# Gated linear attention into a squared-ReLU MoE: the transposes of the last six chunks moved from TensorE to DMAs on SyncE's queue, and a longer lead of the chunks over the MoE

## The chip, the cores and the metric

The kernel runs on one core of a Trainium2 chip. The metric is the device time of one launch in microseconds. Before the change the median of three runs is 194.05 us (193.65 to 194.7). The profiled execution took 194.29 us, and its profile spans 192.3 us from the first to the last instruction.

## The reference

Two stages follow each other. The first is a recurrence per batch and head, over 768 steps; the state is a 48 x 48 matrix:

```python
def _attn_ref(q, k, v, alpha):            # each 4 x 8 x 768 x 48
    state = np.zeros((B, H, D, D))
    for t in range(S):
        state = alpha[:, :, t, :, None] * state + np.einsum('bhd,bhe->bhde', k[:, :, t], v[:, :, t])
        y[:, :, t] = np.einsum('bhd,bhde->bhe', q[:, :, t], state)
    return y
```

Its result, with the heads side by side, is a matrix x of 3072 tokens by 384. The second stage is

```python
    h = x @ w_in                          # 384 x 2048
    r = np.maximum(h, 0.0)
    out = (r * r) @ w_out                 # 2048 x 384
```

Inputs and output are float32. alpha lies between 0.8 and 1.

## The kernel before

**Chunks.** The recurrence is computed in 24 chunks of 128 tokens, six for each batch, in `add_chunk(s)`. Four loads of 192 KB bring alpha, q, k and v of a chunk (line 296). ScalarE (ACT) takes the logarithm of alpha (L, line 318). TensorE (PE) multiplies it by a triangular matrix of ones, which gives cumulative sums, and adds the chunk's totals (`e_p0`, line 326). ACT makes the exponentials A and 1/A of the sums (lines 345 and 349). VectorE (DVE) makes qA = q * A (line 370) and kI = k / A (line 373) in bf16, each 128 tokens by 8 heads padded to 64 columns.

For the scores, channels have to lie on partitions, so qA and kI are transposed: four 128 x 128 transposes on PE for each, into one PSUM bank (`e_p1q`, `e_p1k`, lines 377 to 387, through the helper `tr`, line 223), and one DVE copy of 1024 columns from PSUM into the tile `qkT` (line 397; the first four chunks do it in halves on DVE or ACT). Eight score matmuls follow (`e_p2`, line 402, into the PSUM tile `sc`), DVE masks them in two instructions (line 414, tile `sm`), PE adds the part that comes from the state (`e_p3a`) and the part within the chunk (`e_p3b`, lines 442 to 455), ACT copies the result to bf16 (`xn`, line 463), PE transposes it in three pieces (`e_p4`, line 467), and DVE copies these into `xT_big` (line 474), which holds x transposed for all tokens. From kI, not from its transpose, PE updates the state (`e_ps`, line 420), DVE scales it (line 434) and ACT copies it (line 439). The scratch for L, qA and kI has four buffers (`NBUF`), so a chunk's logarithm waits for the chunk four before to be at its end (`old`, line 305). The loads have six buffers (`LB`): a load waits until the instruction that used its buffer six chunks before is done.

**MoE.** Tokens go in twelve groups (`GN`: 4, 1, 1, then 2 chunks each). For each group and each of 16 slices of d_ff, PE does three matmuls (`add_moe1`; 256 columns for two chunks), ACT the ReLU (line 513) and DVE the square (line 520, tile `gT`). Then for each chunk of the group 16 matmuls of 384 columns in four quarters (`add_moe2`, line 532), a copy by ACT or DVE (`ob`, lines 549 and 551) and a store of 192 KB (line 556). All matmuls stand at line 220, all transposes at line 223, as both go through a helper.

**What sets the order.** Every step is an `Op` with an engine, a duration and a latency that the author wrote down, and its dependences. `Plan.run` (lines 96 to 136) fills the engines in model time: it picks what can start first, and by priority among equals. The resulting list, sorted by start, is emitted in that order, and each engine executes its instructions in that order. PSUM banks are part of the model: two banks go to the chunks (`GLA_BANKS`), two or three to the first MoE matmul, one or more to the second. An operation on PE that depends on another engine gets a slack of 0.25 us in the model once PE is past 25 us (lines 75 to 77). Stores are emitted 3.5 us later than the model's time (`OUT_LATE`), so that they don't hold up SP. Loads and stores are all issued on SyncE's (SP's) queue, in order; the weights come on GpSimd's (POOL's).

How far chunks may run ahead of the MoE is set by `gate` (line 601): a chunk's cumulative sum may be placed when

```python
            return s <= LEAD + (prog["m1"] + prog["m2"]) / 5.12
```

where the fraction is the MoE work placed so far, in chunks, and `LEAD` is 3.5. There are 24 loads of each kind and eight completion semaphores that DMAs on SP take in turn.

Of the kernel before, what the change touches and what calls it, by code (L numbers as in the profile page):

```python
# [9 lines left out]
BF16 = mybir.dt.bfloat16  # L10
# [44 lines left out]
def after(op, x=0.0):  # L55
    return (op, x)


class Plan:
# [36 lines left out]
    def run(self, gate):  # L96
        free = self.free
        while any(self.pending.values()):
            best = None
            for eng, ops in self.pending.items():  # L100
                t0 = free.get(eng, 0.0)
                pick = None
                fifo = eng in ("DMA",)
                for op in (ops[:1] if fifo else ops):
                    if not gate(op):
                        continue
                    r = self.ready(op)
                    if r is None:
                        continue
                    if len(op.durs) > 1:  # L110
                        ends = {e: max(r, free.get(e, 0.0)) + x + LAT[e] for e, x in op.durs.items()}
                        if ends[eng] > min(ends.values()):
                            continue
                    key = (max(r, t0), op.prio)
                    if pick is None or key < pick[0]:
                        pick = (key, op)
                if pick is not None and (best is None or pick[0][0] < best[0]):
                    best = (pick[0][0], eng, pick[1])
            assert best is not None, "nothing can run"
            t, eng, op = best  # L120
            for e in op.durs:
                self.pending[e].remove(op)
            op.eng, op.dur = eng, op.durs[eng]
            op.start = t + getattr(op, "late", 0.0)
            free[eng] = t + op.dur
            if op.lat is None:
                op.lat = LAT.get(eng, 0.2)
            if eng == "OUT":
                free["DMA"] = max(free.get("DMA", 0.0), t) + op.dur
            op.done = t + op.dur + op.lat  # L130
            if op.takes is not None:
                self.ready(op)
                op.slot.release.append(op.gives if op.gives is not None else op)
            self.order.append(op)
            self.on_pick(op)
        self.order.sort(key=lambda o: o.start)
# [3 lines left out]
def kernel(  # L140
# [10 lines left out]
    nc = tc.nc  # L151
    B, H, S, D = q.shape
    HD = H * D
    P = 128
    DP = 64
    NP = H // 2
# [17 lines left out]
    work = ctx.enter_context(tc.tile_pool(name="work", bufs=4))  # L174
# [18 lines left out]
        out=utri_f, in_=utri_f, compare_op=ALU.is_ge, fill=0.0,  # L193
# [20 lines left out]
    xT_big = big.tile([P, KT, n_tok], BF16)  # L214

    def pin(ins):
        tc.keep_in_program_order(ins)
# [4 lines left out]
    def tr(*a):  # L222
        pin(nc.tensor.transpose(*a))  # L223

    plan = Plan()
# [5 lines left out]
    GLA_BANKS = sl_bank[0:2]  # L231
    SIDE_BANKS = sl_bank[2:4]
# [6 lines left out]
    X_SLACK = 0.2  # L239
    LD = 0.93  # L240
    LD_LATE = 1.05
    WLD = 2.05
    SQ_PRIO = 0.0

    def add(eng, dur, emit, *deps, **kw):
        return plan.add(Op(eng, dur, emit, deps, **kw))
# [6 lines left out]
    def load_w(which):  # L253
# [9 lines left out]
        issue = add("POOL", W_ISSUE, e_issue, w_gate[0], prio=-3.0, lat=0.4)  # L263
        w_ready[which].append(add("DMA", WLD * (hi - lo) / 4, lambda: None, issue, lat=2.2))

# [21 lines left out]
    EARLY = 4  # L287

    def add_load(s, nm):
# [7 lines left out]
        prev = C[s - LB]["use_" + nm] if s >= LB else None  # L297
        d["ld_" + nm] = add("DMA", LD if s < 6 else LD_LATE, ld, prev, d.get("go") if nm == "at" else None, lat=2.0 if s < 4 else 2.4, at=0.6)

    def add_chunk(s):  # L300
        d = C[s]
        b, c = divmod(s, NCH)
        i = s % NBUF
        L, qA, kI, ae = L_s[:, i], qA_s[:, i], kI_s[:, i], ae_s[:, i]
        old = C[s - NBUF].get("end") if s >= NBUF else None
        g = dict(prio=-10.0 + s * 0.01)
        last = c == NCH - 1

        def cast(op, out_t, in_t):
            if op.eng == "ACT":  # L310
                pin(nc.scalar.copy(out_t, in_t))  # L311
            elif op.eng == "DVE":
                pin(nc.vector.tensor_copy(out_t, in_t))  # L313
            else:
                pin(nc.gpsimd.tensor_copy(out_t, in_t))
# [58 lines left out]
        mq = d["use_qt"] = add("DVE", 0.47, e_qA, a_, d["ld_qt"], old, **g)  # L374
        mk = d["use_kt"] = add("DVE", 0.47, e_kI, ai, d["ld_kt"], old, **g)
# [6 lines left out]
        def e_p1k():  # L382
            d["pTk"] = psum(p1k, [P, 2 * NP, P], BF16) if s < EARLY else d["pTq"]
            for p in range(NP):
                tr(d["pTk"][:, NP + p, :], kI[:, 2 * p:2 * p + 2, :], ident_bf)
        p1q = plan.add(Op("PE", 0.22, e_p1q, [mq], takes=GLA_BANKS, **g))
        p1k = plan.add(Op("PE", 0.22, e_p1k, [mk, after(p1q)], takes=SIDE_BANKS if s < EARLY else None, lat=0.15, **g))

        def e_cp(lo, hi):
            if lo == 0:  # L390
                d["qkT"] = work.tile([P, 2 * NP, P], BF16, name="qkT")
            cast(cpk if lo else cp, d["qkT"][:, lo:hi, :], (d["pTk"] if lo else d["pTq"])[:, lo:hi, :])
        if s < EARLY:
            cp = add({"ACT": 0.49, "DVE": 0.34}, 0, lambda: e_cp(0, NP), p1q, **g)
            cpk = add({"DVE": 0.34, "ACT": 0.49}, 0, lambda: e_cp(NP, 2 * NP), p1k, **g)
        else:
            cp = cpk = add("DVE", 0.61, lambda: e_cp(0, 2 * NP), p1k, **g)
        p1q.gives = cp
        if s < EARLY:
            p1k.gives = cpk  # L400

# [62 lines left out]
        xn = add("ACT", 0.36, e_xn, p3b, **g)  # L464
        (p3a or p3b).gives = xn

        def e_p4():
            d["px"] = psum(p4, [P, KT, P], BF16)
            for j in range(KT):
                tr(d["px"][:, j, :], d["xn"][:, j * P:(j + 1) * P], ident_bf)  # L470
        p4 = plan.add(Op("PE", 0.165, e_p4, [xn], takes=GLA_BANKS, lat=0.14, **g))

        def e_xT():
            cast(xT, xT_big[:, :, s * P:(s + 1) * P], d["px"])
        xT = add({"ACT": 0.36, "DVE": 0.27} if s < EARLY else "DVE", 0.27, e_xT, p4, prio=-9.0)
        d["x"] = d["end"] = xT
        p4.gives = xT
# [86 lines left out]
    for d in DMA_ORDER + [s for s in range(NT) if s not in DMA_ORDER]:  # L564
        if d in ("i", "o"):
            load_w(d)
        else:
            if d in HOLD_X:
                hold_x(C[d], *HOLD_X[d])
            for s, nm in LOAD_ORDER.get(d, [(d, nm) for nm, _ in srcs]):  # L570
                add_load(s, nm)
            if d == 3:
                add_chunk(2)
            if d != 2:
                add_chunk(d)
            if d in HOLD_W:
                hold_w(C[d], HOLD_W[d])
# [18 lines left out]
                b2 = add_moe2(g, tt, b2, {}, range(NQ), M2_LAST if g >= NG - 2 else M2_BANKS if g < M1_ALT else [sl_bank[4]])  # L596
        sq[(g, "free")] = b2

    LEAD = 3.5

    def gate(op):
        s = getattr(op, "gla", None)
        if s is not None:
            return s <= LEAD + (prog["m1"] + prog["m2"]) / 5.12
        return True
# [54 lines left out]
```

## Time and profile before

| what | value |
|---|---|
| median of three runs | 194.05 us (193.65 to 194.7) |
| profiled execution | 194.29 us, span 192.3 us, granted TensorE clock 1.00 |
| PE busy | 182.8 us, 95% of the span, 1951 matmuls and transposes |
| DVE busy | 135.2 us, 70%, 367 instructions |
| ACT busy | 126.8 us, 66%, 362 instructions |
| POOL busy | 36.6 us, 19% |
| q and k halves copied from PSUM by DVE, 1024 columns | 20 of 688 ns |
| x copied from PSUM by DVE | 23 of 352 ns |
| DMA on SP's queue | 24 loads of each of alpha, q, k, v, and 24 stores |

The profile is one execution, taken by the hardware profiler. PE is TensorE's matmuls (transposes among them), PEld its weight loads, which run beside the matmuls. L220 is line 220 of the kernel. "Busy" counts the time in which at least one instruction of the engine is under way; matmuls are pipelined, so the duration listed for one is longer than the distance from its start to the next one's. The chain is followed back from the last instruction: at each step to what released it, or to the instruction before it on the same engine. "SPq" is SP issuing DMAs. The time from issue to landing runs from the start of the issuing instruction to the moment the data is there. The loads end at about 125 us; the last chunk's transposes run at 171 us.

### The profile page before, as it was taken

The numbers are of one execution on the slowest core, as the hardware profiler recorded it, in microseconds if no ns is written. First come the engines' busy times: TensorE is split into PE (matmuls) and PEld (weight loads), VectorE is DVE, ScalarE is ACT, GpSimd is POOL, SyncE is SP. The second block draws the span as 40 slices with busy tenths as digits, with TensorE's granted clock in tenths as the row PEclk, the third lists the DMA queues.
The fourth block names the chain that finished last, engine by engine and source line by source line (L and its number), as shares of the span: only waits on it lengthen the run. The fifth ranks groups of instructions, "written<-read, shape, count | busy, mean of one in ns | idle before, by whom it ended". The sixth has DMA issues, their size and how long they took to land.

```text
span 192.3 us, 5252 instructions
## 1 busy us (share of the span) xinstructions
PE 182.8 (95%) x1951; PEld 131.7 (68%) x1952; DVE 135.2 (70%) x367; ACT 126.8 (66%) x362; POOL 36.6 (19%) x71
## 2 busy tenths in 40 slices
PE   7896999998999999999999999999999999999993
PEld 2564654566886787777777867777877877777761
DVE  0787766158999799779878777677878788754410
ACT  3584689147896696977875875766777764746620
POOL 5226900022171213212201110202211100000000
PEclk9999999999999999999999999999999999999999
DMA  6998999999999998989989999671011011011112
GB/s 119 210 208 150 184 204 203 187 203 196 256 174 202 201 210 159 200 169 211 198 177 204 192 217 215 134 178 46 0 44 41 5 41 41 3 41 44 41 41 82
DMA packets 107032, 27.07 MB, mean 141 GB/s; under 512 B 100352, under 2 KB 107008, under 8 KB 107008
## 3 DMA queue, kind: packets, MB, share of 16 engines
q1 hardware_dynamic: 103296, 23.60, 57.2%
q0 software_dynamic: 3712, 3.15, 10.7%
q8 instruction: 15, 0.25, 0.5%
q14 instruction: 9, 0.07, 0.1%
HBM read 25.17 MB, written 4.72 MB: 155 GB/s over the span
## 4 chain that ended last, share of the span: by engine, by line
PE 80%; DMA 6%; SPq 5%; DVE 4%; ACT 3%; issue 1%; POOL 0%; ACTq 0%
PE bank L220 69%; PE bank L223 6%; SPq L296 5%; DMA w_in_b<-in_moe_w_in_dram 3%; PE sc L220 3%; DMA qt<-in_q_dram 2%; ACT r L513 2%; PE st L220 1%; DVE gT L520 1%; ACT ob L551 1%; DVE sm L414 1%; DVE qkT L313 1%; DVE qA_s L370 1%; DVE ob L549 0%; DVE kI_s L373 0%
## 5 line engine op out<-in xcount | busy, mean ns | idle before, releaser
L513 ACT ACTIVATE r<-bank 128x256 bf16<-128x256 f32 (+3 forms) x196 | 69.0, 389 | 24.8 <-PE bank L220 21.8
L220 PE MATMUL bank<-xT_big,w_in_b 128*128 128x256 bf16 (+3 forms) x587 | 80.3, 270 | 0.8 <-ACT r L513 0.3
L220 PE MATMUL bank<-w_out_b,gT 128*128 128x384 bf16 x384 | 74.5, 326 | 0.3 <-ACT ob L551 0.2
L520 DVE TENSOR_TENSOR gT<-r 128x256 bf16<-128x256 bf16 (+3 forms) x196 | 50.7, 290 | 19.6 <-ACT r L513 18.4
L220 PEld LDWEIGHTS <-w_in_b 128*128 128x128 bf16 x588 | 49.2, 97 | 13.9 <-issue 1.9
L220 PEld LDWEIGHTS <-gT 128*128 128x128 bf16 x384 | 36.5, 98 | 17.3 <-issue 0.5
L414 DVE TENSOR_TENSOR sm<-sc,utri_b 128x512 bf16<-128x512 f32 x48 | 30.9, 684 | 5.6 <-PE sc L220 5.4
L323 POOL CAST vb<-vt 128x384 bf16<-128x384 f32 x24 | 17.9, 745 | 51.2 <-PE bank L220 21.2
L370 DVE TENSOR_TENSOR qA_s<-qt,A 128x384 bf16<-128x384 f32 x24 | 13.8, 573 | 14.8 <-ACT A L345 14.6
L356 POOL TENSOR_TENSOR ae_s<-ae,halves_t 128x8 f32<-128x8 f32 x24 | 9.6, 401 | 69.2 <-ACT ae L353 52.7
L313 DVE COPY qkT<-bank 128x1024 bf16<-128x1024 bf16 (+1 forms) x25 | 15.9, 635 | 4.2 <-PE bank L223 3.5
L318 ACT ACTIVATE L_s<-at 128x384 bf16<-128x384 f32 x24 | 12.9, 536 | 8.2 <-DMA at<-in_alpha_dram 8.2
L311 ACT CAST xn<-bank 128x384 bf16<-128x384 f32 x24 | 11.6, 485 | 9.3 <-PE bank L220 9.2
L220 PEld LDWEIGHTS <-qkT 64*128 64x128 bf16 (+1 forms) x272 | 10.8, 95 | 9.9 <-DVE gT L520 3.2
L345 ACT ACTIVATE A<-bank 128x384 bf16<-128x384 f32 x24 | 11.9, 496 | 7.7 <-PE bank L220 7.6
L551 ACT COPY ob<-bank 128x384 f32<-128x384 f32 x21 | 10.1, 482 | 10.0 <-PE bank L220 9.9
L373 DVE TENSOR_TENSOR kI_s<-kt,Ainv 128x384 bf16<-128x384 f32 x24 | 14.2, 593 | 0.0
L349 ACT ACTIVATE Ainv<-bank 128x384 bf16<-128x384 f32 x24 | 12.2, 507 | 0.0
L434 DVE TENSOR_TENSOR st<-st,ae_s 128x384 f32<-128x384 f32 x20 | 11.1, 556 | 0.2 <-PE st L220 0.2
L220 PE MATMUL bank<-warm 128*128 128x256 bf16 (+1 forms) x52 | 10.0, 320 | 1.3 <-DVE halves_t L210 1.3
L439 ACT CAST sb<-st 128x384 bf16<-128x384 f32 x20 | 9.6, 478 | 1.6 <-DVE st L434 1.5
L220 PE MATMUL sc<-qkT 64*128 64x128 bf16 x192 | 9.5, 219 | 0.7 <-DVE qkT L313 0.3
(43 smaller groups left out, 136.5 us busy)
## 6 DMA issues: line engine op xcount, KB each, us to landing
at<-in_alpha_dram SPq DMA_DIRECT2D x24, 192.0 KB, 4.0
qt<-in_q_dram SPq DMA_DIRECT2D x24, 192.0 KB, 4.0
kt<-in_k_dram SPq DMA_DIRECT2D x24, 192.0 KB, 4.0
vt<-in_v_dram SPq DMA_DIRECT2D x24, 192.0 KB, 4.0
out_dram<-ob SPq DMA_DIRECT2D x24, 192.0 KB, 2.6
w_in_b<-in_moe_w_in_dram POOLq DMA_DIRECT2D x4, 384.0 KB, 6.9
w_out_b<-in_moe_w_out_dram POOLq DMA_DIRECT2D x4, 384.0 KB, 11.0
```

Source lines behind the costliest of these rows:

```text
L220: pin(nc.tensor.matmul(*a, **kw))
L313: pin(nc.vector.tensor_copy(out_t, in_t))
L318: pin(nc.scalar.activation(L[:, :, 0:D], d["at"], AF.Ln))
L323: pin(nc.gpsimd.tensor_copy(d["vb"], d["vt"]))
L345: pin(nc.scalar.activation(d["A"], d["pm"][:, 0:HD].rearrange("p (h d) -> p h d", h=H), AF.Exp))
L349: pin(nc.scalar.activation(d["Ai"], d["pm"][:, 0:HD].rearrange("p (h d) -> p h d", h=H), AF.Exp, scale=-1.0))
L370: pin(nc.vector.tensor_mul(qA[:, :, 0:D], d["qt"], d["A"]))
L373: pin(nc.vector.tensor_mul(kI[:, :, 0:D], d["kt"], d["Ai"]))
L414: pin(nc.vector.tensor_mul(d["sm"][:, hh], d["sc"][:, hh], utri_b.to_broadcast([P, NP, P])))
L513: pin(nc.scalar.activation(box["r"][:, 0:n], box["ph"][:, 0:n], AF.Relu))
L520: pin(nc.vector.tensor_mul(gT[g][:, f, lo * P:lo * P + n], box["r"][:, 0:n], box["r"][:, 0:n]))
L551: pin(nc.scalar.copy(box["ob"], box["po"]))
```

## The change

For chunks 18 to 23, qA, kI and xn are no longer transposed by TensorE. SyncE issues a transposing DMA (`dma_start_transpose`) for each: qA into the first half of `qkT`, kI into the second, xn directly into its columns of `xT_big`. PE's eleven transposes of these chunks go, and with them the PSUM banks they took and DVE's copies. In the model the DMAs have an engine of their own, "XB", with a duration of 0.6 us, a latency of 2.4 and a lateness of 1.0 that delays their place in the emitted order and their end; they also take time from the model's DMA queue. `LEAD` goes from 3.5 to 5.5 for all chunks.

```diff
@@ Plan.run
-            if eng == "OUT":
+            if eng in ("OUT", "XB"):
                 free["DMA"] = max(free.get("DMA", 0.0), t) + op.dur
-            op.done = t + op.dur + op.lat
+            op.done = t + op.dur + op.lat + (op.late if eng == "XB" else 0.0)
...
+    XB_FROM = 18
+    XB = 0.6
+    XB_LAT = 2.4
+    XB_LATE = 1.0
...
@@ add_chunk
-        p1q = plan.add(Op("PE", 0.22, e_p1q, [mq], takes=GLA_BANKS, **g))
-        p1k = plan.add(Op("PE", 0.22, e_p1k, [mk, after(p1q)], takes=SIDE_BANKS if s < EARLY else None, lat=0.15, **g))
+        def e_xb(lo):
+            if lo == 0:
+                d["qkT"] = work.tile([P, 2 * NP, P], BF16, name="qkT")
+            pin(nc.sync.dma_start_transpose(out=d["qkT"][:, lo:lo + NP, :], in_=(kI if lo else qA).rearrange("p h d -> p (h d)")))
+
+        def e_xx():
+            pin(nc.sync.dma_start_transpose(out=xT_big[:, :, s * P:(s + 1) * P], in_=d["xn"]))
+        xb = s >= XB_FROM
+        if xb:
+            cp = add("XB", XB, lambda: e_xb(0), mq, prio=-5.0, lat=XB_LAT)
+            cpk = add("XB", XB, lambda: e_xb(NP), mk, after(cp), prio=-5.0, lat=XB_LAT)
+            cp.late = cpk.late = XB_LATE
+        p1q = None if xb else plan.add(Op("PE", 0.22, e_p1q, [mq], takes=GLA_BANKS, **g))
+        p1k = None if xb else plan.add(Op("PE", 0.22, e_p1k, [mk, after(p1q)], takes=SIDE_BANKS if s < EARLY else None, lat=0.15, **g))
...
-        if s < EARLY:
+        if xb:
+            pass
+        elif s < EARLY:
...
-        p4 = plan.add(Op("PE", 0.165, e_p4, [xn], takes=GLA_BANKS, lat=0.14, **g))
+        p4 = None if xb else plan.add(Op("PE", 0.165, e_p4, [xn], takes=GLA_BANKS, lat=0.14, **g))
...
+        if xb:
+            d["x"] = d["end"] = add("XB", XB, e_xx, xn, prio=-9.0, lat=XB_LAT)
+            d["x"].late = XB_LATE
+            return
...
-    LEAD = 3.5
+    LEAD = 5.5
```

## The prediction

> **What bounds the kernel now.** I read the page first, for who is busy and when; then the busy time by stretches, because an average hides stages; then the chain in order of time, for what one chunk costs the bounding engine; last the DMA rows, because the change moves work there.
>
> From the page (busy share of each engine, then 40 slices of 4.8 us in tenths, then the chain that ended last):
>
> ```profile
> PE 182.8 (95%) x1951; PEld 131.7 (68%) x1952; DVE 135.2 (70%) x367; ACT 126.8 (66%) x362; POOL 36.6 (19%) x71
> ...
> PE   7896999998999999999999999999999999999993
> ...
> DMA  6998999999999998989989999671011011011112
> ...
> PE 80%; DMA 6%; SPq 5%; DVE 4%; ACT 3%; issue 1%; POOL 0%; ACTq 0%
> ```
>
> TensorE (PE) is the bound from about 45 us to the end, and the DMA engines are full until about 125 us and nearly idle afterwards. By stretches (us, then busy us and count of PE, weight loads, DVE, ACT, POOL; clock, DMA share, GB/s):
>
> ```profile
> 65.00:75.00 10.00, 9.68 (x136) 8.01 (x129) 9.95 (x29) 8.98 (x29) 3.07 (x4) 1.00 0.97 210
> ...
> 125.00:135.00 10.00, 10.00 (x115) 7.19 (x113) 7.62 (x19) 6.21 (x17) 0.96 (x2) 1.00 0.40 107
> 135.00:145.00 10.00, 10.00 (x115) 7.79 (x111) 7.95 (x22) 8.09 (x24) 1.98 (x4) 1.00 0.06 21
> 145.00:155.00 10.00, 10.00 (x114) 7.50 (x113) 8.22 (x24) 6.89 (x20) 0.51 (x1) 1.00 0.06 22
> ```
>
> From 125 us, where chunks 18 to 23 lie, PE never rests, DVE has 20% to spare and the DMA engines over 90%. The one stretch where DVE is full (9.95 of 10) is also one where PE rests. Now the chain inside a chunk (start, us, what; all of it PE, so a TensorE instruction taken out there shortens the end):
>
> ```profile
> 136.49 0.17 PE bank L223 x3
> 136.66 0.66 PE bank L220 x6
> 137.32 0.22 PE bank L223 x4
> 137.54 1.12 PE bank L220 x7
> 138.66 0.22 PE bank L223 x4
> 138.88 0.17 PE st L220 x4
> 139.05 1.30 PE bank L220 x10
> 140.36 0.33 PE sc L220 x8
> ```
>
> L223 is the transpose helper: three for x (of the chunk before), four for q, four for k; then the state update, ten MoE matmuls, the score matmuls. The costs of a DMA on SP's queue, duration of the issue and time from issue to landing (ns and us; the loads of alpha, then the stores of the output):
>
> ```profile
> L296 SPq DMA_DIRECT2D at<-in_alpha_dram x24: 368/796/2797, 0.8 to 119.1; - x24
> DMA to landing us min/median/max: 2.8/4.0/6.4
> ```
>
> ```profile
> L556 SPq DMA_DIRECT2D out_dram<-ob x24: 332/448/1557, 43.9 to 189.5; - x24
> DMA to landing us min/median/max: 1.8/2.6/5.1
> ```
>
> **The change part by part.** Base: this profiled execution took 194.29 us (span 192.3 and 2.0 around it), 0.24 above the median of 194.05. A measurement of this kernel can tell about 0.5%, 1.0 us, from no change.
>
> 1. Transposes off TensorE. Six chunks lose 4 + 4 + 3. In the chain a group of four takes 0.22 and one of three 0.17, so 0.61 a chunk and 3.66 in all. The other end: L223's own busy time is 1.10 us per 7 us stretch, 6.6 in six, but a matmul's listed 219 ns runs beside its successor, so start to start is nearer and I take 3.66. The weight loads that go with them (98 ns) run beside the matmuls already. Minus 3.66.
>
> 2. The evictions: six 1024-column copies at 688 ns and six 384-column ones at 352 ns leave DVE, 6.2 us. By the built order two output evictions also move from DVE (557 ns) to ACT (482). DVE has 20% free there: nothing. The waits of PE's weight loads for the q/k copy are 3.4 us in all, but 0.3 after 76 us. Nothing.
>
> 3. Waiting for q and k. Order now: DVE makes qA, then kI; SP issues the q half, then the k half; both must land before the score matmuls. Behind the score matmuls on PE everything queues, in order, so a late half costs its lateness in each of six chunks. The cover is what the built order puts between the state update (which needs kI, like the DMA) and the score matmuls. For chunk 20, at the rates of the chain: the update 0.17, fifteen MoE1 matmuls (0.33 for 3, 0.65 for 6) 1.6, twelve MoE2 (0.65 for 4) 1.95, the next chunk's cumulative sum 0.28 (69.64 to 69.92 in the timeline), together 4.0 us; for chunk 19 it is 3.9, for chunk 18 4.7, for 21 and 22 3.9 and 4.3. The code asks for as much: ready plus 0.6 + 2.4 + 1.0, and 0.25 of slack on PE. The trace shows no transposing DMA. Bounds from the nearest rows: from 2.6 (a store on the quiet queue) over 4.0 (median load on a full queue) to 6.4 (slowest load). A half carries 128 KB, a load or store 192 KB. For chunks 20 to 23 the queue holds stores only, so the store's row is nearest: 2.6 plus 0.2 for the q issue still running is 2.8, under 4.0; no stall. For 18 and 19 loads are still in flight and one load of v stands between the two halves: 18 gets 0.8 + 4.0 = 4.8 against 4.7, 19 with the v load as the last on the queue 0.4 + 4.0 = 4.4 against 3.9. Plus 0.6. Ends: minus nothing (both under cover), and for six chunks at 6.4 + 0.2 against 4.0, plus 15.6.
>
> 4. The x transposes: landing may take 6.4 us, but the MoE that reads it comes up to 5.5 chunks of 6 us later, and what waits for it besides (line 305's old: the logarithm of chunk s+4) runs 19 us before its exponentials (chunk 22: 137.4 and 156.9). Nothing; without that cover, a full landing per chunk.
>
> 5. SP's queue: 18 more issues. The v load of chunk 22 and the four of 23 stand behind transposes that wait for qA and kI; chunk 23 is needed some 25 us later. Stores stand behind x transposes that wait for xn; six output buffers cover that. The issues cost SP's sequencer 18 x 0.8 = 14 us of some 45, in which the built order has six stores besides. Nothing; at 2.8 us each (the longest alpha issue) 50 us, and the queue itself would be the bound.
>
> 6. The lead. PE's order is unchanged up to the score matmuls at 74.1 us; from there chunk 11 and on come earlier, by two chunks in the end. TensorE's work is the same, but DVE, which does about 3.8 us per chunk (products 1.1, scores' mask 1.3, copies 0.95, state 0.5), gets chunks 11 to 14 in 4.5 us each besides the squares. The 68.8 to 74.1 stretch has this already: 5.3 us of chain on ACT and DVE, PE busy 5.00 of 5.30, 0.30 lost. Two more such stretches at most 0.6, none at least; I take one, plus 0.35 with the waits after it. It might also gain: less waiting at 95 to 115 us (PE 9.84 and 9.86 of 10), up to minus 0.3.
>
> Sum: 194.29 - 3.66 + 0.6 + 0.35 = 191.6 against the profiled execution, 191.3 against the median.
>
> What the Trainium skill says of the unknown. "VectorE: DVE Perf Modes", section The three transpose paths, gives 1309 ns for 128x128 in bf16 by the DMA crossbar and 390 ns by TensorE, and so speaks against the change; the row here is 0.22 us for four on TensorE, 55 ns each. If the blocks went one after another, a chunk's eleven would need 14.4 us (an estimate from that page) against a chunk period of 6.3, six chunks 86 us from about 115, and with the last MoE group's 13.5 us behind them the end would be near 215 us. "Advanced Engine Details and Errata", X-Bar Transpose (TRN2), has crossbar transposes as fast as ordinary DMAs, 350 to 400 GB/s, 0.35 us for a half; by it the sum is 191.0 against the profiled execution, without the 0.6. No run here shows either yet.
>
> **The rivals.**
> - *Slower: the score matmuls wait for the k half in every chunk.* For it: it is the only new wait that PE has in order, the 4 us cover is no more than a median load's landing, and two issues stand in series on SP. Against it: smaller transfers, an empty ring after 125 us. It decides when kI to landing exceeds about 4.5 us (4.0 + 3.3/6). At 5.5 us: 194.05 - 3.3 + 6 x 1.5 = 199.7; at 6.6: 206.
> - *About the same: the lead outruns the loads.* Issues of alpha stand at 73.5, 78.4, 82.6 and 87.6 us (chunks 13 to 16), 4.4 to 5 us apart, and land 4 later. Chunk 14's products run at 99.8 us now; two chunks of 7 earlier is 85.8, where its k lands at about 84.5 and its v at 85.3 (issues at 80.6 and 81.3). If each of chunks 12 to 14 waits 1.1 us the gain is eaten: 194.05 - 3.66 + 3.3 = 193.7. Against it: PE's order stretches the pull over four chunks.
> - *Hidden anyway*, the freed time passing to DVE: against it the 20% of DVE that is free from 125 us, and more after the change. Counted with the one before.
>
> **How the numbers follow.** Gain as summed 0.62, with its own range 189.7 (no stall, the lead gaining 0.3: 190.1, and 0.4 for the spread of the runs shown) to 192.9 (a second full DVE stretch 0.3, chunks 18 and 19 later by another 0.65, 0.65 for the spread); slower rival 0.28, nearly all beyond plus 1 us, 0.03 within; the loads 0.10, shared 0.02 faster, 0.04 same, 0.04 slower. So faster 0.63, same 0.08, slower 0.29. The top of the range takes in the slower rival to 199.0 (kI to landing about 5.4 us); half of it, and a little below 189.7, stays out.
>
> **What would show it.** L223 with 66 matmuls fewer (264 to 198) and a chain still on PE from 125 us; issues of transposes on SP with landing under 4 us; "PE sc" idle under 0.3 us before each of the last six score groups. Wrong if PE idles before the score matmuls of chunks 18 to 23 released by a DMA, or idles between 75 and 95 us released by DVE or ACT by over 1 us, or if the transposes' issues alone fill SP.

## The result and the profile after

The changed kernel takes 192.31 us (median of 20 runs, 191.41 to 194.14) against 194.29 us (20 runs). The ratio is 0.991, with an interval of 0.989 to 0.993: faster by 2.0 us between the medians, by 1.3 to 2.1 us by the interval. The profiled execution took 191.97 us, its span is 190.1 us; before it was 194.29 and 192.3, so the two traces differ by 2.3 us.

The page of the changed kernel, with the same lines as before: busy shares, 40 slices, the chain.

```profile
PE 180.5 (95%) x1885; PEld 128.6 (68%) x1886; DVE 128.7 (68%) x353; ACT 126.7 (67%) x364; POOL 33.5 (18%) x71
...
PE   7998999998999999999999999998999999999992
...
DMA  6997999999999899999999995499243331211212
...
PE 74%; DMA 12%; SPq 5%; POOL 3%; DVE 2%; ACT 1%; issue 1%; ACTq 0%
```

TensorE (PE) has 66 instructions fewer and is still the bound. The DMA engines, at 40% from 125 to 135 us before and nearly idle afterwards, are now at 88% there, at 47% and 32% in the next two stretches, and at 11 to 23% after 155 us. The stretches (us, then busy us and count of PE, PEld, DVE, ACT, POOL, clock, DMA share, GB/s):

```profile
75.00:85.00 10.00, 9.81 (x123) 7.79 (x120) 9.91 (x30) 8.69 (x29) 2.56 (x4) 1.00 1.01 199
85.00:95.00 10.00, 10.00 (x129) 7.53 (x127) 9.63 (x25) 7.10 (x22) 2.66 (x5) 1.00 0.97 199
...
115.00:125.00 10.00, 10.00 (x103) 7.50 (x97) 7.02 (x21) 7.53 (x23) 0.73 (x2) 1.00 0.54 110
125.00:135.00 10.00, 9.08 (x106) 6.87 (x106) 7.74 (x21) 7.58 (x23) 1.56 (x4) 1.00 0.88 141
135.00:145.00 10.00, 10.00 (x106) 7.35 (x105) 7.01 (x21) 7.85 (x24) 0.50 (x1) 1.00 0.47 100
```

DVE is full for longer (75 to 95 us) and PE hardly rests in it. One stretch has lost much PE time: 125 to 135 us. The chain there, in order of time, shows one foreign piece, the k half of chunk 19:

```profile
126.85 0.17 PE st L220 x4
127.02 4.60 DMA qkT<-kI_s
131.62 0.05 issue
131.67 0.40 PE sc L220 x8
```

PE itself stands for 0.92 us of these 4.6 ("[0.92 <-DMA qkT<-kI_s]" at the scores of 131.67 in its timeline). What stood before that half on SP's queue (start, us of the issue; in this kernel L300 are the loads, L393 the q and k transposes, L396 those of x, L579 the stores):

```profile
124.42 0.43 SPq L300 DMA_DIRECT2D kt<-in_k_dram  x1
124.96 1.34 SPq L393 DMA_TRANSPOSE qkT<-qA_s  x1
126.40 0.53 SPq L300 DMA_DIRECT2D vt<-in_v_dram  x1
127.02 1.52 SPq L393 DMA_TRANSPOSE qkT<-kI_s  x1
128.63 2.02 SPq L396 DMA_TRANSPOSE xT_big<-xn  x1
```

The v load of chunk 23 was issued between the halves of chunk 19. It stands there because SP issues in order: from 114.44 to 119.00 us SP waited for qA of chunk 18 to issue that chunk's q half, and the v load of chunk 22 and the four loads of chunk 23 came behind it. From 115 to 125 us the DMA engines moved 110 GB/s, against 177 before. On a quiet queue a transpose lands sooner than the model's 4.0 us; the longest landing here, 4.6, is that of the half above (L393, duration of the issue in ns, and issue to landing in us):

```profile
L393 SPq DMA_TRANSPOSE qkT<-kI_s x6: 1188/1216/1894, 121.0 to 153.5; - x6
DMA to landing us min/median/max: 2.3/2.5/4.6
```

**A balance of PE.** In the trace of before, each form of matmul has a usual distance to the next start after 75 us: 109 ns for 256 columns, 162 for 384, 56 for a transpose. Adding up what each distance has over the usual one for its form gives PE's lost time. From 65 us on it is 5.6 us before and 6.8 after. So the trace has 66 x 56 ns = 3.7 us of transposes less and 1.2 us of losses more, 2.5 in sum, and the last output copy does start 2.5 us earlier (189.03 and 186.52). Of the 1.2 us, 1.1 lie before the scores of chunk 19. The same sum is used for the kernels below.

### The profile page after: what moved, and what is told of

Read it like the earlier page. It is cut to its first block, busy times and chain, and to the rows that moved or that the text cites. A ratio compares the mean times of both kernels' runs of the same rounds, so it can differ in the third digit from the quotient of the medians.

```text
span 190.1 us, 5150 instructions
## 1 busy us (share of the span) xinstructions
PE 180.5 (95%) x1885; PEld 128.6 (68%) x1886; DVE 128.7 (68%) x353; ACT 126.7 (67%) x364; POOL 33.5 (18%) x71
## 4 chain that ended last, share of the span: by engine, by line
PE 74%; DMA 12%; SPq 5%; POOL 3%; DVE 2%; ACT 1%; issue 1%; ACTq 0%
PE bank L220 65%; DMA w_out_b<-in_moe_w_out_dram 6%; SPq L300 5%; PE bank L223 4%; PE sc L220 3%; DMA qt<-in_q_dram 3%; DMA qkT<-kI_s 2%; POOL w_in_b L264 2%; PE st L220 1%; POOL w_out_b L266 1%; DVE sm L433 1%; POOL vb L327 1%; ACT r L536 1%; DVE gT L543 0%; DVE qA_s L374 0%
## 5 line engine op out<-in xcount | busy, mean ns | idle before, releaser
L220 PE MATMUL bank<-w_out_b,gT 128*128 128x384 bf16 x384 | 73.7, 326 | 0.4 <-DMA w_out_b<-in_moe_w_out_dram 0.4
L543 DVE TENSOR_TENSOR gT<-r 128x256 bf16<-128x256 bf16 (+3 forms) x196 | 51.7, 295 | 24.4 <-ACT r L536 20.9
L220 PEld LDWEIGHTS <-w_in_b 128*128 128x128 bf16 x588 | 49.8, 97 | 15.4 <-issue 2.2
L360 POOL TENSOR_TENSOR ae_s<-ae,halves_t 128x8 f32<-128x8 f32 x24 | 10.7, 444 | 86.7 <-ACT ae L357 79.3
L574 ACT COPY ob<-bank 128x384 f32<-128x384 f32 x23 | 11.1, 482 | 13.1 <-PE bank L220 13.0
L327 POOL CAST vb<-vt 128x384 bf16<-128x384 f32 x24 | 14.0, 586 | 23.3 <-DMA vt<-in_v_dram 9.3
L377 DVE TENSOR_TENSOR kI_s<-kt,Ainv 128x384 bf16<-128x384 f32 x24 | 13.5, 564 | 0.2
L317 DVE COPY qkT<-bank 128x1024 bf16<-128x1024 bf16 (+1 forms) x19 | 11.6, 614 | 1.8 <-PE bank L223 1.6
L220 PE MATMUL bank<-warm 128*128 128x256 bf16 (+1 forms) x52 | 10.8, 341 | 1.3 <-DVE halves_t L210 1.3
```

The source lines that it names most:

```text
L220: pin(nc.tensor.matmul(*a, **kw))
L327: pin(nc.gpsimd.tensor_copy(d["vb"], d["vt"]))
L377: pin(nc.vector.tensor_mul(kI[:, :, 0:D], d["kt"], d["Ai"]))
L543: pin(nc.vector.tensor_mul(gT[g][:, f, lo * P:lo * P + n], box["r"][:, 0:n], box["r"][:, 0:n]))
```

## The experiments

The theory at this point: PE is the bound, the transposes taken off it are worth 56 ns each, the one wait in chunk 19 comes from the load in front of it, and the lead gains nothing by itself. The rivals: the gain is the lead's; or the transposes' own latency is what PE waits for, and the load has no part in it. All ratios are to the kernel before, measured beside each.

**The lead alone** (the transposes stay on PE):

```diff
-    XB_FROM = 18
+    XB_FROM = 24
```

> All transposes stay on TensorE, the lead is 5.5. Theory (TensorE is the bound, each transpose taken off it is worth its 56 ns of start-to-start time, and the lead only decides where the chunks' work stands): the same TensorE work as before, so 194.0 to 194.7 against 194.3, nothing beyond 0.3%. Rival (the lead fills idle stretches and is the larger part of the gain): 192.3 to 193.

Measured: 195.31 us against 194.46, ratio 1.004 (1.002 to 1.006). The lead by itself costs 0.4%. The profiled execution took 194.49 us, the fastest of the twelve. In it PE's lost time rises from 5.6 to 6.3 us, not in the stretch where DVE is full but at the end, where no chunk is left to fill in. Twice PE waits there for the copy of an output; from the chain after 160 us:

```profile
161.12 0.49 ACT ob L574
...
161.65 14.01 PE bank L220 x102
...
175.69 0.49 ACT ob L574
```

So the gain isn't the lead's. The cost is a little over the 0.3% that was allowed for, and the place is another than the one priced. The trace is of the shortest execution, so it need not hold all of the 0.8 us between the medians.

**The transposes alone:**

```diff
-    LEAD = 5.5
+    LEAD = 3.5
```

> Transposing DMAs for chunks 18 to 23, the lead stays 3.5. Theory: TensorE loses 3.7 us, but with 3.5 chunks of MoE work in hand at the end the two landings of the last chunk (2.4 us for the k half, 2.3 us for x) and the longer way between them stand closer to the end; the last MoE groups wait, and much of the gain goes back as TensorE idle in the last 25 us: 193 to 196. Rival (the transposes gain by themselves, the lead is not needed; the loads are over by then, so not even chunk 19 waits): 190.5 to 191.

Measured: 196.53 us against 194.46, ratio 1.010 (1.007 to 1.012). Slower than before, with 66 transposes fewer on PE, and 0.5 us above the range that was expected. The profiled execution took 195.03 us, 1.5 less than the median, so the trace holds the smaller part of the loss only. Its loads are over before the transposes start, no k half is waited for, and PE still loses 9.9 us after 65 us, 4.3 more than before, all of it after 135 us. With 3.7 us of transposes less that makes plus 0.6; the other 1.5 us of the median are in no trace. The chain near the end:

```profile
180.66 0.50 PE bank L220 x3
181.17 0.02 issue
181.19 0.39 ACT r L536
181.58 0.04 issue
181.62 0.50 PE bank L220 x3
```

Three first-stage MoE matmuls, then the ReLU that frees their PSUM bank, again and again: 0.96 us for two groups of three that otherwise take 0.65. The last chunk's x comes late (its scores, then the transpose of x, landing at 174.9 us; before, DVE copied it at 171.4, and in the changed kernel it lands at 163.4). By then the second-stage matmuls that PE mixes in between are used up, and the first stage alone runs at the pace of the ReLU that frees its banks. This is what the lead is for; a lead of 4.5, below, comes out between. Neither half of the change gains; together they do.

**The load out of the way** (k and v of chunk 23 are issued behind the k half of chunk 19):

```diff
+            d["kT"] = cpk
...
-        d["ld_" + nm] = add("DMA", LD if s < 6 else LD_LATE, ld, prev, d.get("go") if nm == "at" else None, lat=2.0 if s < 4 else 2.4, at=0.6)
+        d["ld_" + nm] = add("DMA", LD if s < 6 else LD_LATE, ld, prev, d.get("go") if nm == "at" else None,
+                            after(C[19]["kT"]) if s == 23 and nm in ("kt", "vt") else None, lat=2.0 if s < 4 else 2.4, at=0.6)
```

> The changed kernel, but the loads of k and v of chunk 23 are issued behind the k half of chunk 19. Theory (the 1.1 us for which TensorE stands before the scores of chunk 19 come from the v load in front of the k half, and from the full queue, which make its landing 4.6 us instead of 2.4): the wait goes, 191.2 against the changed kernel's 192.3; the k half of chunk 19 lands within 3 us. Rival (the cover of 3.9 us is too short for a transpose at that place whatever is in front of it): 192.3, the wait stays at 0.8 to 1.1 us.

Measured: 190.82 us against 194.46, ratio 0.982 (0.978 to 0.985). The same kernel a second time:

> The kernel with the k and v loads of chunk 23 behind the k half of chunk 19, once more, beside the next two: 190.5 to 191.2, no wait of TensorE on a k half.

190.87 against 193.96, ratio 0.986 (0.981 to 0.990). The wait is gone, PE's lost time is back at 5.8 us in both traces, 1.0 less than with the change. The stretch of the wait in the second of them:

```profile
125.00:135.00 10.00, 10.00 (x114) 7.69 (x114) 8.13 (x22) 7.88 (x25) 1.58 (x4) 1.00 0.78 152
```

One part of the expectation missed: the k half did not land within 3 us but 4.3 us after its issue, with a store and the q half still in flight (landing at 127.92 and 128.44). What helped most is the earlier issue: 0.3 us after kI was ready, not 1.4 (at 126.11, not 127.02). It landed at 130.40, with the scores at 130.87: 0.5 us to spare. So the rival was half right: with a cover of 3.9 us, counted from kI, PE would still have waited 0.7 us.

**The change once more**, beside other kernels:

> The changed kernel once more, beside the others: 192.0 to 192.6 against 194.3 to 194.5, with the wait of 0.8 to 1.2 us before the scores of chunk 19. If it came out at the time of the kernel with the k and v loads of chunk 23 behind (190.8), the difference between the two would have been the chip's.

192.33 us against 194.09, ratio 0.988 (0.985 to 0.992), with 1.23 us of waiting before the same scores. One of the six runs took 190.16 us; the trace is of another. The medians lie some 1.5 us above those of the kernel with the loads moved. The two kernels were not run beside each other, though: by the ratios to the kernel before (0.991 and 0.988 against 0.982 and 0.986) the distance is 0.5 to 1.9 us, and the intervals of the second pair overlap. That the wait goes is shown in the traces. What that brings in time is known no closer than this range, which the 0.9 to 1.2 us that PE stood there fit.

**A shorter cover** (the order is made as if a transpose landed 2 us sooner):

```diff
-    XB_LAT = 2.4
+    XB_LAT = 0.4
```

> The changed kernel, but the order is made as if a transpose landed 2 us sooner (latency 0.4 in place of 2.4), so the score matmuls stand 2 us earlier in TensorE's order. Theory (the k half is there some 2.5 us after kI on a quiet queue and 5 to 6 on the full one, so the cover is what hides it): TensorE waits before the scores of all six chunks, about 0.5 us each for 20 to 23, 1.5 for 18 and 3 for 19, 196 to 198. Rival (the cover has slack to spare, and the wait in chunk 19 is of another kind): 192.3 to 193.4, no wait before the scores of chunks 20 to 23.

Measured: 197.57 us against 194.46, ratio 1.016 (1.012 to 1.020). PE waits before the scores of all six chunks (waits of PE, total us, times, longest):

```profile
PE sc L220 <- DMA qkT<-kI_s: 6.2, 6, 2.5
```

The cover is what hides the transposes. The edit did more than was meant: SP's order now has the x transpose of the chunk before between the two halves, so the waits of chunks 20 to 23 hold its 1.2 us of issue as well, and the split by chunk isn't as expected. And the longest wait costs more than its length. In the columns of the stretches above:

```profile
130.00:132.00 2.00, 0.10 (x1) 0.00 (x0) 0.26 (x1) 0.30 (x1) 0.00 (x0) 1.00 0.50 115
132.00:134.00 2.00, 1.43 (x17) 0.97 (x18) 0.99 (x2) 0.48 (x1) 0.00 (x0) 0.74 0.27 98
134.00:136.00 2.00, 2.00 (x12) 1.30 (x11) 1.30 (x4) 1.22 (x5) 0.21 (x1) 0.50 0.00 0
```

After 2.5 us of idleness the granted clock is 0.50 for 3.4 us (from 132.95 to 136.36), and by the balance PE loses another 1.5 us in it.

**Transposes among the loads** (from chunk 12 on):

```diff
-    XB_FROM = 18
+    XB_FROM = 12
```

> Transposing DMAs from chunk 12 on, not 18. Theory (a transpose that shares the queue with loads lands 4 to 5 us after its issue instead of 2.4, and the planner's 4.0 us do not cover that; each also takes about 0.7 us of the DMA engines, which are full until the loads end): another 3.7 us of TensorE work goes, but chunks 12 to 19 wait about 1 us each before their scores and the loads come later: 191 to 196, with 5 to 9 us of waits on the k halves. Rival (chunk 19 was a single collision; the queue can take more): no waits beyond one, 188 to 189.

Measured: 198.81 us against 194.09, ratio 1.022 (1.018 to 1.025), outside the range that was given, on its slow side. Another 66 transposes are gone from PE, and it loses 18.0 us instead of 5.6 (waits of PE; then two stretches):

```profile
PE sc L220 <- DMA qkT<-kI_s: 8.2, 8, 2.0
```

```profile
95.00:105.00 10.00, 7.42 (x77) 4.96 (x75) 5.41 (x15) 5.82 (x18) 1.00 (x2) 1.00 0.80 157
...
155.00:165.00 10.00, 7.74 (x62) 5.03 (x61) 3.78 (x10) 4.35 (x14) 0.66 (x2) 0.83 0.69 148
```

The waits on k halves are the 5 to 9 us expected, but not for the reason given: these halves land 2.3 to 3.4 us after their issue, not 4 to 5. It is the issue that is late. kI of chunk 15 was ready at 96.66 us, and its k half was issued at 101.72: SP had loads, a store, an x transpose and the q half in front of it. Of the other 4 us of losses, 1.6 come from a clock of 0.50 for 3.4 us, again behind a pause of 2 us, and 1.4 from PE's waits for the ReLU, for x and for an output copy. The loads suffer as well: from 75 to 165 us the DMA engines carry 148 to 185 GB/s instead of some 200, and the last load lands at 159 us instead of 131.

**x alone, earlier** (x from chunk 8, q and k from 18, loads of chunk 23 moved):

```diff
+    XX_FROM = 8
...
-        p4 = None if xb else plan.add(...)
+        p4 = None if s >= XX_FROM else plan.add(...)
...
-        if xb:
+        if s >= XX_FROM:
             d["x"] = d["end"] = add("XB", XB, e_xx, xn, prio=-9.0, lat=XB_LAT)
```

> The kernel with the k and v loads of chunk 23 behind, and in addition x alone (not q and k) by transposing DMAs from chunk 8 on: ten more x transposes leave TensorE, 0.17 us each. Theory (x is needed chunks later, so its landing is covered even on a full queue, and the loads have slack): 189.1 against 190.8. Rival (the DMA engines are full there, and ten transposes of 0.5 to 0.7 us make the loads of chunks 12 to 16 late, which the longer lead needs early): 191 to 193, with TensorE idle between 70 and 100 us.

Measured: 196.98 us against 194.09, ratio 1.010 (1.006 to 1.015); some 6 us more than without the edit, and above what the theory and the rival gave. The profiled execution took 198.14 us, 1.2 more than the median, so I read it for places only. The worst place, on SP's queue and then on PE:

```profile
72.53 3.50 SPq L398 DMA_TRANSPOSE xT_big<-xn  x1
76.15 1.59 SPq L301 DMA_DIRECT2D kt<-in_k_dram  x1
...
78.59 0.82 PE L220 MATMUL bank<-xT_big,w_in_b 128*128 128x256 bf16 x6 [2.02 <-DMA xT_big<-xn]
```

One transpose, x of chunk 9, holds SP for 3.5 us and lands 6.0 us after its start, and between 76 and 78 us the DMA engines move 15 GB/s. The cover that the theory counted on is not there: the first MoE matmul that reads this x stands 4.0 us behind the issue, so PE waits 2.0 us, and behind that pause the clock is 0.50 for 3.4 us (1.6 us lost by the balance). Nor is it only that a transpose lands late in a full queue: the loads behind it aren't issued meanwhile, and the engines run dry. The last load is issued at 144.75 us, not at about 130, so that loads now stand in front of the k halves of chunks 18 to 21, and PE waits for these 4.4 us in all. Whether the issue waits for the queue to empty or for something else was not settled.

**The size of the lead**, both with the loads of chunk 23 moved:

```diff
-    LEAD = 5.5
+    LEAD = 4.5      # and 6.5
```

> The kernel with the k and v loads of chunk 23 behind, with a lead of 4.5 chunks instead of 5.5. Theory (the lead buys the MoE work that TensorE mixes in at the end; alone it costs up to 0.8 us, at 3.5 the last groups' first matmuls stand alone and wait for the ReLU): between 190.8 and 3.5's 196.5, nearer to the first, 191 to 193, with waits of the first MoE matmuls on the ReLU in the last 25 us. Rival (one chunk more than before is enough): 190.3 to 190.8.

> The same kernel with a lead of 6.5 chunks. Theory (at 5.5 TensorE has no waits left in the last 25 us, so more lead has nothing to give, and it draws chunks closer to their loads): 190.8 to 192. Rival (the lead goes on giving as from 3.5 over 4.5 to 5.5): under 190.3.

4.5: 192.11 us against 194.09, ratio 0.990 (0.987 to 0.994), within the range expected, but the waits are for the copies of outputs (1.2 us), not the ReLU. 6.5: 192.41 against 193.96, ratio 0.993 (0.990 to 0.996), above it. It isn't a clean test of the lead: with the chunks earlier, the v load of chunk 23 falls between the halves of chunk 20 (q 127.99, v 129.36, k 129.98 us), and the 0.74 us wait of PE is back at that place. It shows the collision a second time, one chunk further.

**Twice the transposes of x** (the second into a scratch tile, loads of chunk 23 moved):

```diff
+            dup = work.tile([P, KT, P], BF16, name="dup")
+            pin(nc.sync.dma_start_transpose(out=dup, in_=d["xn"]))
```

> The same kernel; each x transpose of chunks 18 to 23 is issued a second time, into a scratch tile that nothing reads. Theory (on the quiet queue a transpose's 1.2 us on SP and its some 0.7 us of the DMA engines lie beside other work, and only what TensorE waits for in order counts): 190.6 to 191.3, as without. Rival (SP's queue is near its limit with transposes of 1.2 us; one more per chunk delays the next q and k halves): over 192.5, with waits on the k halves of chunks 20 to 23.

Measured: 190.63 us against 193.96, ratio 0.983 (0.978 to 0.987): the same as without. Six more DMAs on the quiet queue cost nothing.

## Why the prediction was right

The direction and the range held: 191.3 us was given, 192.31 measured. The range reached to 199.0 us, past the time before the change, but the gain's own range, 189.7 to 192.9, holds the result too. The gain was forecast at 2.75 us and came out at 2.0 between the medians (1.3 to 2.1 by the interval, 2.3 in the profiled executions). Point by point:

1. *Transposes off TensorE, minus 3.66.* 66 instructions at 56 ns, 3.7 us. Right; the other end, 6.6 us from the busy time, would have been wrong, as the listed 219 ns of a matmul runs beside the next.
2. *Evictions, nothing.* PE shows no wait on them after the change. Right.
3. *Waiting for q and k, plus 0.6.* The mechanism and the place were right: one wait, in chunk 19, behind the v load; none in 20 to 23, where the k halves land 2.3 to 3.0 us after issue. This is the term that was mis-sized: 0.92 and 1.23 us of waiting in two traces. I had 0.1 for chunk 18 (none) and 0.5 for 19. The step that failed took the issue of a transpose for that of a store or load, 0.2 to 0.8 us; it is 1.2, 1.3 to 1.5 in the busy queue, so the k half was issued 1.4 us after kI, and it landed after 4.6 us, not 4.0. What softened it is that kI was there 5.1 us, not 3.9, before PE reached the scores: it was done 1.2 us before the state update, from which I counted. Two errors that partly cancel are luck.
4. *x, nothing.* Right for chunks 18 to 23, and the doubled x transposes confirm that the quiet queue has room. The x from chunk 8 shows both conditions: among the loads one x landed after 6.0 us, near the 6.4 that I allowed for, and the cover of several chunks did not exist at chunk 9, where the MoE reads x 4.0 us later.
5. *SP's queue, nothing.* Right as a sum, though the 18 issues took 24.2 us and not 14. Wrong at one place: the loads behind the transposes of chunk 18, which I had named and put at nothing, are those that then stand in front of the k half of chunk 19.
6. *The lead, plus 0.35, in the stretch where DVE is full.* The trace of the change has 0.15 us more loss from 65 to 115 us. The lead alone costs 0.8 us, though, and its trace has the losses at the end: a place that the step didn't price. With the transposes on the DMA that end runs without it (0.2 us lost after 165 us, 0.4 before). Why the output copies are waited for in the one and not in the other was not tried.

What the prediction missed about the lead is its use: I priced it as a cost and said nothing of the transposes without it, which are 1% slower than before. Its terms would have given about 191 us for the transposes alone, where 196.53 was measured. So the forecast was right for the pair, and in part by luck: its parts don't add up one by one.

Of the signs that it named, two failed, both in chunk 19 alone: the two halves landed 4.3 and 4.6 us after issue, not under 4, and PE stood more than 0.3 us before the scores. It also called any wait for a DMA before these scores a sign of being wrong, while its own sum had 0.6 us there. The slower rival, late k halves in every chunk, is real but needs a shorter cover or a fuller queue: it is what the shorter cover and the transposes among the loads measure. Whether another engine's queue would have kept the k halves free of the loads was not tried. The rival by the loads did not show: no wait of PE on a load after 65 us.

Of the two pages of the Trainium skill that differed, "Advanced Engine Details and Errata", X-Bar Transpose (TRN2), came nearer with transposes as fast as ordinary DMAs: 128 KB land 2.3 us after the issue on the quiet queue (a median of 2.5 for the six k halves), a store of 192 KB after a median of 2.4. The 1309 ns of "VectorE: DVE Perf Modes", The three transpose paths, cannot be the price of each of four blocks in a row, which would be 5.2 us (an estimate from that page).

## What to carry to other kernels

A transpose on the DMA cost little here where the queue was quiet and the consumer was placed 4 us behind in the bound engine's order. It cost much between loads: there the issuing queue, which works in order, held up the loads behind the transposes and the transposes behind the loads. So count from the moment the data is ready to the landing, and not from the issue alone. Latency that is moved onto a path must be paid for with work in hand at the end of the kernel, so test the two halves of such a change separately before one is dropped. And where one wait is left, look at the queue in front of it: moving two loads behind one transpose took the wait away and brought the time to 190.8 us, a gain of 1.4 to 1.8% instead of 0.9 to 1.2%.

## What was not expected of the hardware

- The issue of a transposing DMA keeps SP's sequencer for 1.2 us even when the queue is empty (1.18 to 1.22 in 12 of the 18); a load's takes 0.4 to 0.6 there. The other six took 1.3 to 2.0 us, four of them while loads were in flight and two after the last one. With the shorter cover one behind a load took 2.5 us, and in the kernel with x from chunk 8 one took 3.5, while DMA throughput fell to 15 GB/s.
- TensorE's granted clock fell to 0.50 after pauses of 2.0 (twice) and 2.5 us, for 3.4 us each time, beginning 0.4 to 1.1 us after TensorE had started again. It lost another 1.5 to 1.6 us in that, so such a pause costs 1.6 to 1.8 times its length. Pauses of 0.90 to 1.66 us left it at 1.00. The page "TensorE: Matmul & The Clock Gate" of the Trainium skill, Part 1, has an idle window of about 3.4 us; here less was enough.
